# Another order for the first transfers on SyncE's queue in an attention and two-layer gated network kernel

## The chip, the cores and the metric

The kernel runs on one core of a Trainium2 chip. The time is the device time of one execution in microseconds (us); where several runs of a kernel are given, it is their median.

## What is computed

Attention over 4 batches of 8 heads (576 tokens, head size 64) with a block-causal mask, then a gated layer, then a mixture of four experts weighted by given probabilities. All inputs lie in the chip's memory; the three weights of the gated layer come as 64-bit floats and are turned into 32-bit ones on the chip.

```python
scores = scale * np.matmul(q, k.transpose(0, 1, 3, 2))
scores = np.where(mask, scores, -1000000000.0)         # blocks of 64, block_i >= block_j
scores = scores - np.max(scores, axis=-1, keepdims=True)
attn = np.exp(scores)
attn = attn / (np.sum(attn, axis=-1, keepdims=True) + 1e-09)
x = np.matmul(attn, v)                                 # (4, 8, 576, 64) -> (2304, 512)
gate = 1.0 / (1.0 + np.exp(-(x @ w_gate)))
x = gate * (x @ w_val) @ w_out
for e in range(4):
    out += p[:, e:e + 1] * (np.maximum(x @ w1[e], 0.0) @ w2[e])
```

## The kernel before, in words

TensorE does the products. Each 32-bit weight or activation is split into a high and a low part (`split_sb`, line 123), and three products of parts stand for one, so that a weight takes work on ScalarE, VectorE and GpSimd before TensorE can use it.

**Attention.** A batch has four pairs of heads. `attn_items` (line 151) writes the attention as one list of small steps, pair after pair. For a pair, `prep_tr` (line 220) transposes q and k on TensorE (lines 225, 233, 258), `s_begin` makes a score block (line 345), VectorE writes the mask and takes the row maximum (lines 375, 376; 406 and 408 for the last, short row block), ScalarE takes the exponentials (lines 378, 411), `p_tr` transposes them on TensorE (line 454) with ScalarE taking them out of PSUM (line 441), and `pv_both` multiplies with v into the tile `obank` (line 118, the helper that records these products) and stores the result (lines 532, 536).

**Weights of the gated layer.** They come in twelve groups of 128 columns. `conv_items` (line 628) gives twelve steps for a group: two loads of a raw block of 512 KB each (`raw`, line 634, one of `w_gate`, one of `w_val`), two conversions (`f64`, lines 601 on ScalarE, then 602 and 603 on VectorE), and then sums on GpSimd (line 649), splits (lines 128, 130, 132) and stores of the converted parts (line 657). The raw blocks have three buffers. Five groups (`NC0`, line 19) are converted while the attention of the first batch runs.

**Who loads what.** Nearly all transfers are issued by SyncE, one after the other, in the order in which the program writes them; an issue that has to wait for a buffer holds those behind it. ScalarE issues only the first pair's q. `load_first` (line 169) loads the first pair's q and k, with the last 64 tokens of both in two transfers of their own (line 176). `loads(g)` (line 203) loads the q and k of pair g in six transfers, and `load_v(g)` (line 207) its v in three (lines 195 and 199).

**What sets the order.** `attn_to(A00)` (lines 1283 and 1287) first writes the attention's list up to 12% of the first batch. `_merge` (line 43) then writes the rest of that batch and the weights' steps in alternation, so that both advance evenly. When the program has been written out, the compile step orders the instructions of each engine with a time model of its own (`TC_ARGS`, line 38): an instruction written later can go ahead of one whose inputs the model expects later. On the chip each engine runs its instructions in that fixed order. In the program of before, the first item of the list (line 552) issues `load_first`, `load_v(0)` and `loads(1)`; `load_v(1)` follows among the items up to 12%, and the raw blocks come only with `_merge`.

Of the kernel before, what the change touches and what calls it, by code (L numbers as in the profile page):

```python
# [18 lines left out]
NC0 = 5  # L19
# [9 lines left out]
PT2_BUFS = 1  # L29
LT, LP = 3, 4  # L30
PTB = 3
EARLY = True
HB = 19
W2B = 4
FIRSTP = 1
# [7 lines left out]
def _merge(a, b, pace=1.0):  # L43

    ta = sum(c for c, _ in a) or 1.0
    tb = sum(c for c, _ in b) or 1.0
    i = j = 0
    ca = cb = 0.0
    while i < len(a) or j < len(b):
        if j >= len(b) or (i < len(a) and pace * ca / ta <= cb / tb):  # L50
            c, fn = a[i]
            i += 1
            ca += c
        else:
            c, fn = b[j]
            j += 1
            cb += c
        fn()
# [3 lines left out]
def attention_moe_moe_kernel(  # L62
# [17 lines left out]
    E, _, F2 = w1.shape  # L80
# [3 lines left out]
    NF = DFF // P  # L84
# [66 lines left out]
    def attn_items(segs):  # L151
# [3 lines left out]
        items = []  # L155
# [4 lines left out]
        def nat_of(g):  # L160
            return pairs[g][3] != "F"

        def kts_of(g):
            return KTS[pairs[g][3]]
# [4 lines left out]
        def load_first():  # L169
            q0 = nat[0, "q"] = attn.tile([P, 5, 2, D], F32, tag="qn", name="qn")  # L170
            k0 = nat[0, "k"] = attn.tile([P, 5, 2, D], F32, tag="kn", name="kn")
            for c in range(4):
                for e, t, z in ((nc.scalar, q0, q), (nc.sync, k0, k)):
                    e.dma_start(out=t[:, c], in_=z[0, 0:2, c * P:(c + 1) * P, :].rearrange("h p d -> p h d"))
            for x, z in enumerate((k, q)):
                nc.sync.dma_start(
                    out=k0[64 * x:64 * x + 64, 4], in_=z[0, 0:2, 512:S, :].rearrange("h p d -> p h d"))

        def load(g, nm, src, c0, c1):
            _, b, pr, seg = pairs[g]  # L180
            if nm == "v":
                t = vts[g % 2]
            elif nat_of(g):
                if nm == "k" and pr % 2:
                    t = attn.tile([P, 5 * P], F32, tag="tk", name="kn", bufs=3)
                    t = t.rearrange("p (c h d) -> p c h d", c=5, h=2)
                else:
                    tag = "kn" if nm == "k" else ("qn", "vn")[pr % 2]
                    t = attn.tile([P, 5, 2, D], F32, tag=tag, name=f"{nm}n")
            else:  # L190
                t = attn.tile([P, 5, 2, D], F32, tag=f"{nm}n", name=f"{nm}n")
            nat[g, nm] = t

            for x, (y, z) in enumerate(((nm, src),) if nm == "v" else (("k", k), ("q", q)) if nm == "k" else ()):
                nc.sync.dma_start(
                    out=t[64 * x:64 * x + 64, 4], in_=z[b, 2 * pr:2 * pr + 2, 512:S, :].rearrange("h p d -> p h d"))
            cc = min(c1, 4)
            for h in range(2):
                nc.sync.dma_start(
                    out=t[:, c0:cc, h, :],  # L200
                    in_=src[b, 2 * pr + h, c0 * P:cc * P, :].rearrange("(c p) d -> p c d", p=P))

        def loads(g):
            load(g, "q", q, 0, 4)
            load(g, "k", k, 0, max(kts_of(g)) + 1)

        def load_v(g):
            load(g, "v", v, 0, max(kts_of(g)) + 1)
# [329 lines left out]
        def prep_list(g):  # L538
            seg = pairs[g][3]
            r = [(False, 0.0, lambda: prep_alloc(g))]  # L540
            for nm, cs in (("q", range(4)), ("k", KTS[seg])):
                for part in ([c for c in cs if c < 2], [c for c in cs if c >= 2]):
                    if part:
                        r.append((False, 110.0 * len(part), lambda nm=nm, part=part: prep_tr(g, nm, part)))
            return [(g, *x) for x in r]
# [3 lines left out]
        def later(s, *its):  # L549
            extra.setdefault(s, []).extend(its)  # L550

        items.append((0, False, 0.0, lambda: (load_first(), load_v(0), *((loads(1),) if EARLY and nat_of(1) else ()))))
        items += prep_list(0)
        for g in range(len(pairs)):
            if g == 0:
                continue
            base, per = start[g - 1], start[g] - start[g - 1]
            if g > 1 or not (EARLY and nat_of(1)):
                later(base, (g, False, 0.0, lambda g=g: loads(g)))
            later(base + per // 2, (g, False, 0.0, lambda g=g: load_v(g)))  # L560
            pl = prep_list(g)
            for m, it in enumerate(pl):
                later(min(base + per // 2 + (m * (per - 1 - per // 2)) // max(len(pl) - 1, 1), start[g] - 1), it)
# [31 lines left out]
    def from_f64(bits, out=None):  # L595

        lo, hi = bits[:, :, 0], bits[:, :, 1]
        f = lo if out is None else out.bitcast(I32)  # L600
        nc.scalar.activation(out=hi.bitcast(F32), in_=hi.bitcast(F32), func=AF.Prelu, scale=2.0 ** -112, alpha=2.0 ** 32)
        nc.vector.tensor_scalar(out=f, in0=lo, scalar1=29, scalar2=None, op0=ALU.logical_shift_right)  # L602
        nc.vector.scalar_tensor_tensor(  # L603
            out=f, in0=hi, scalar=3, in1=f, op0=ALU.logical_shift_left, op1=ALU.bitwise_or)
        return f.bitcast(F32)
# [19 lines left out]
    def w1_at(f, k):  # L625
        return wc_d[f][:, WAT[k][0] * QF:WAT[k][1] * QF].rearrange("p (h n f) -> p h n f", h=2, f=QF)

    def conv_items(f):

        d = {}  # L630

        def raw(gv):
            t = d["raw", gv] = conv.tile([P, NKT, P, 2], I32, tag="raw", name="raw", bufs=3)
            nc.sync.dma_start(
                out=t.rearrange("p c f t -> p c (f t)"),
                in_=(w_gate, w_val)[gv].bitcast(I32)[:, 2 * f * P:2 * (f + 1) * P].rearrange("(c p) f -> p c f", p=P))

        def f64(gv):
            d[gv] = from_f64(d["raw", gv].rearrange("p c f t -> p (c f) t"))

        def b(k, a):
            return d[a][:, k * QF:(k + 1) * QF]

        def sums(n):
            if n == 0:
                d["t"] = conv.tile([P, 4, QF], F32, tag="wt", name="wt")
            t = d["t"]
            x, y = [(b(0, 1), b(0, 0)), (b(1, 1), t[:, 0]), (b(1, 1), b(0, 1)), (b(1, 0), t[:, 1])][n]
            nc.gpsimd.tensor_tensor(out=t[:, n], in0=x, in1=y, op=ALU.subtract)

        def part(k):
            t = w1_tile(k)
            src = dict(a=lambda: d[0], b=lambda: d["t"][:, 0:2].rearrange("p n f -> p (n f)"),
                       c=lambda: d["t"][:, 2:4].rearrange("p n f -> p (n f)"), d=lambda: b(1, 1))[k]()
            split_sb(t[:, 0].rearrange("p n f -> p (n f)"), t[:, 1].rearrange("p n f -> p (n f)"), src,
                     "p" if k in "bc" else "a", "v" if k == "a" else "p")
            nc.sync.dma_start(out=w1_at(f, k), in_=t.bitcast(F32))
            if f >= NC0 - 1:
                wg[f, k] = t

        r = [lambda: raw(0), lambda: raw(1), lambda: f64(0), lambda: f64(1), lambda: sums(0), lambda: part("a"),
             lambda: sums(1), lambda: part("b"), lambda: sums(2), lambda: sums(3), lambda: part("c"), lambda: part("d")]
        return [(1.0, x) for x in r]
# [231 lines left out]
    if True:  # L895
# [380 lines left out]
        def attn_next():  # L1276
            queue[pos[0]][3]()
            pos[0] += 1
            if pos[0] == len(queue):
                pt2.release()  # L1280
                attn.release()

        def attn_to(target):
            while pos[0] < len(queue) and place[pos[0]] < target:
                attn_next()

        attn_to(A00)
        a0 = [(queue[i][2], attn_next) for i in range(pos[0], len(queue)) if place[i] < A1[0]]
        cs = [conv_items(f) for f in range(NF)]
        _merge(a0, sum(cs[:NC0], []), 1.0)  # L1290
        x_items = x1_prep(0)
        prev = []
        for p in range(NP1):
            at, total = 0.0, NF * 7 * 6 * C1 + NF * 2 * NKT * 3 * C1
            for f0 in range(0, NF, 2):
# [5 lines left out]
                items = []  # L1301
# [31 lines left out]
                if f0 == 0 and p < 2:  # L1333
                    items = x_items + items
# [22 lines left out]
        for p in range(NPASS):  # L1357
            for q0 in range(0, NQ, 2):
                last = p == NPASS - 1 and q0 == NQ - 2
                items = l1_items(p, q0) + l1_items(p, q0 + 1)  # L1360
                if (p, q0) == (0, 0):
                    m = len(items) // 2
                    items = [items[m * (c == "B") + "1526743".index(x)] for c, x in
                             ("A1", "A2", "A5", "B1", "A6", "B2", "A7", "B6", "B5", "A4", "B7", "A3", "B4", "B3")]
# [19 lines left out]
                if q0 == 0 and p:  # L1384
                    items = x_items[4:] + items
                if q0 == NQ - 2 and p + 1 < NPASS:
                    x_items = x_prep(p + 1)
                    items = x_items[:4] + items
# [41 lines left out]
```

## Time and profile before

| | us |
|---|---|
| median of 3 runs | 1418.28 |
| lowest and highest of them | 1415.96, 1418.3 |
| the profiled execution, its own time | 1414.19 |
| its span from first to last instruction | 1412.4 |
| TensorE busy in it | 1369.8 (97%) |
| VectorE busy | 981.4 (69%) |
| ScalarE busy | 780.9 (55%) |
| GpSimd busy | 505.2 (36%) |

In the rows PE is TensorE, PEld its weight loads, DVE VectorE, ACT ScalarE, POOL GpSimd and SP SyncE; a q behind the name (SPq) means the issuing of a transfer. L601 is line 601 of the kernel. "[3.28 <-DMA raw]" behind an instruction means that its engine had stood idle for 3.28 us until that transfer landed. Busy shares over the whole span say little about the opening, with which this change deals; it is read by stretches.

### The profile page before, as it was taken

How to read it: one execution, taken by the hardware profiler on the slowest of the kernel's cores; microseconds unless marked ns; L12 is line 12 of the kernel's file. 1: busy time of each engine (PE TensorE's matmuls, PEld its weight loads, DVE VectorE, ACT ScalarE, POOL GpSimd, SP SyncE). 2: the span in 40 equal slices, each digit the busy share in tenths (PEclk: the TensorE clock that was granted, in tenths of full speed). 3: DMA queues.
4: the chain of work that ended last, by engine and by line, in shares of the span. 5: the costliest groups of instructions: out<-in, count | busy, mean ns of one | idle time of the engine just before them, and what ended most of it. 6: DMA issues, size and time to landing. Idle time of an engine off the chain costs nothing.

```text
span 1412.4 us, 26270 instructions
## 1 busy us (share of the span) xinstructions
PE 1369.8 (97%) x9192; PEld 1264.0 (89%) x9192; DVE 981.4 (69%) x2111; ACT 780.9 (55%) x1926; POOL 505.2 (36%) x538
## 2 busy tenths in 40 slices
PE   5889998999999999999999999999999999999998
PEld 3447787888899999999999989999999999999998
DVE  6868689986666545567777666757766787766766
ACT  5878888888876433443445445444444454443442
POOL 4544357531112100022576556533322342322322
PEclk8999999999999999999999999999999999999999
DMA  8989787867656887898799888886666777776754
GB/s 230 314 239 297 224 262 253 261 197 211 214 183 227 305 298 264 291 368 306 270 333 359 295 304 298 293 297 237 232 245 247 254 263 282 245 270 229 277 203 157
DMA packets 213682, 371.91 MB, mean 263 GB/s; under 512 B 75568, under 2 KB 140080, under 8 KB 207408
## 3 DMA queue, kind: packets, MB, share of 16 engines
q1 hardware_dynamic: 212464, 369.99, 77.6%
q8 instruction: 73, 1.20, 0.3%
q14 instruction: 57, 0.47, 0.1%
q10 hardware_dynamic: 1088, 0.26, 0.1%
HBM read 269.00 MB, written 101.19 MB: 262 GB/s over the span
## 4 chain that ended last, share of the span: by engine, by line
PE 83%; DVE 6%; ACT 4%; DMA 3%; issue 1%; POOL 1%; SPq 1%; DVEq 0%; ACTq 0%; POOLq 0%
PE c L118 36%; PE o L118 26%; PE lo L118 6%; PE s L118 4%; PE obank L118 3%; PE t L118 3%; PE tbank L454 2%; PE s L345 1%; DMA raw<-in_moe_w_gate_dram 1%; DVE raw L602 1%; ACT pt L378 1%; DVE raw L603 1%; PE tbank L225 1%; DVE nm L376 1%; ACT pTb L441 1%
## 5 line engine op out<-in xcount | busy, mean ns | idle before, releaser
L118 PE MATMUL c<-xc,w1g 128*128 128x384 f32 x1920 | 384.8, 338 | 1.0 <-DMA w1g<-w1d 0.7
L118 PEld LDWEIGHTS c<-xc,w1g 128*128 128x128 f32 x1920 | 330.5, 188 | 7.5 <-issue 0.9
L118 PE MATMUL o<-w2s,hb 128*128 128x256 f32 x1728 | 243.5, 282 | 1.1 <-DVE acc L1207 1.1
L118 PEld LDWEIGHTS o<-w2s,hb 128*128 128x128 f32 x1728 | 231.8, 189 | 2.0 <-DVE acc L1207 1.7
L1067 POOL TENSOR_TENSOR hs<-hf 128x384 f32<-128x384 f32 x64 | 64.1, 1022 | 287.6 <-ACT hf L1075 256.5
L1207 DVE SCALAR_TENSOR_TENSOR acc<-o,pr_t,acc 128x256 f32<-128x256 f32 x264 | 123.5, 479 | 57.8 <-PE o L118 55.5
L118 PE MATMUL lo<-g,wo 128*128 128x288 f32 x888 | 147.2, 299 | 2.8 <-DVE x L880 2.8
L118 PE MATMUL o<-w,hb 128*128 128x512 f32 x576 | 142.9, 391 | 0.0
L118 PEld LDWEIGHTS lo<-g,wo 128*128 128x128 f32 x888 | 126.1, 188 | 6.6 <-DVE x L880 3.7
L1075 ACT ACTIVATE hf<-c 128x384 f32<-128x384 f32 x128 | 65.7, 514 | 114.3 <-DVE c L1112 57.6
L118 PEld LDWEIGHTS o<-w,hb 128*128 128x128 f32 x576 | 107.2, 188 | 18.5 <-DVE acc L1151 0.2
L1112 DVE TENSOR_TENSOR c<-c,snap 128x384 f32<-128x384 f32 x144 | 77.9, 553 | 55.7 <-PE c L118 36.5
L1105 ACT ACTIVATE snap<-c 128x384 f32<-128x384 f32 x144 | 65.8, 485 | 87.4 <-PE c L118 87.2
L1056 ACT ACTIVATE hb<-hs 128x384 fp32r<-128x384 f32 x128 | 63.3, 518 | 64.1 <-POOL hs L1067 64.0
L430 POOL TENSOR_SCALAR pt<-pt,nm 128x128 f32<-128x128 f32 (+4 forms) x72 | 47.3, 663 | 129.4 <-DVE nm L427 95.3
L1058 DVE TENSOR_TENSOR hb<-hs,hb 128x384 fp32r<-128x384 f32 x128 | 87.1, 695 | 5.5 <-ACT hb L1056 5.2
L880 DVE TENSOR_TENSOR x<-lo,x 128x288 f32<-128x288 f32 x124 | 55.6, 452 | 42.2 <-PE lo L118 41.7
L118 PE MATMUL c<-xc,wa 128*128 128x288 f32 x504 | 82.9, 299 | 2.1 <-ACT r L826 1.3
L378 ACT ACTIVATE pt<-s,nm 128x128 f32<-128x128 f32 (+3 forms) x128 | 67.6, 530 | 14.4 <-DVE nm L376 11.6
L118 PEld LDWEIGHTS c<-xc,wa 128*128 128x128 f32 x504 | 71.3, 188 | 4.2 <-ACT r L826 1.6
L118 PE MATMUL c<-xc,wc 128*128 128x288 f32 x432 | 71.1, 299 | 1.5 <-ACT snap L804 1.5
L454 PE MATMUL tbank<-ident,pt 128*128 128x128 f32 x320 | 55.1, 287 | 16.9 <-ACT pTa L441 9.6
(173 smaller groups left out, 2711.1 us busy)
## 6 DMA issues: line engine op xcount, KB each, us to landing
w1g<-w1d SPq DMA_DIRECT2D x96, 512.0 KB, 5.3
w2s<-w2d SPq DMA_DIRECT2D x48, 1024.0 KB, 6.3
w1d<-w1g SPq DMA_DIRECT2D x48, 512.0 KB, 5.3
wa<-w1d SPq DMA_DIRECT2D x40, 512.0 KB, 5.2
wb<-w1d SPq DMA_DIRECT2D x40, 512.0 KB, 5.4
wc<-w1d SPq DMA_DIRECT2D x40, 512.0 KB, 4.3
wo<-wod SPq DMA_DIRECT2D x36, 512.0 KB, 5.7
wr<-in_moe_w_dram SPq DMA_DIRECT2D x32, 512.0 KB, 5.5
```

What stands on the lines that cost most here:

```text
L118: ins = nc.tensor.matmul(out=out, lhsT=lhsT, rhs=rhs, start=start, stop=stop, skip_group_check=skip)
L378: ins = nc.scalar.activation(out=pt[:, x * nk:(x + 1) * nk], in_=sp[:, x - x0], func=AF.Exp, bias=nm[:, j0 + x:j0 + x + 1], scale=1.0, acc ...
L430: nc.gpsimd.tensor_scalar(out=p, in0=p, scalar1=nm[:, 2 + x:3 + x], scalar2=1.0, op0=ALU.mult, op1=ALU.mult)
L454: nc.tensor.transpose(out=tbank[:, x * P:(x + 1) * P], in_=pt[:, x * P:(x + 1) * P], identity=ident)
L880: nc.vector.tensor_tensor(out=x2[t, dm], in0=ps, in1=x2[t, dm], op=ALU.add)
L1056: nc.scalar.activation(out=t[:, 0], in_=src, func=AF.Copy if low is None else AF.Relu)
L1058: nc.vector.tensor_tensor(out=t[:, 1], in0=src, in1=t[:, 0].bitcast(F32), op=ALU.subtract)
L1067: nc.gpsimd.tensor_tensor(out=o, in0=x, in1=y, op=op)
L1075: nc.scalar.activation(out=hf[q, blk], in_=c, func=AF.Relu)
L1105: nc.scalar.activation(out=t, in_=d["c1"][:, :TH], func=AF.Copy)
L1112: nc.vector.tensor_tensor(out=c, in0=d[tag][:, :TH], in1=d[n], op=ALU.add)
L1207: nc.vector.scalar_tensor_tensor(out=o, in0=ps, scalar=pr, in1=o, op0=ALU.mult, op1=ALU.add)
```

## The change

Line 552 is split in two items: `load_first` alone, and then `loads(1)` with `load_v(0)` behind it instead of ahead. Between the two the two raw blocks of the first weight group are issued, and behind the second the first raw block of the second group. These three steps are then left out of the list that `_merge` distributes (57 steps instead of 60). The switch `EARLY` goes; it was on, so `loads(1)` stays where the first item was. SyncE's queue therefore begins with: the first pair's keys and last tokens, two raw blocks, the second pair's q and k, the first pair's v, a third raw block.

```diff
-        items.append((0, False, 0.0, lambda: (load_first(), load_v(0), *((loads(1),) if EARLY and nat_of(1) else ()))))
+        items.append((0, False, 0.0, load_first))
+        items.append((0, False, 0.0, lambda: (loads(1), load_v(0))))
...
-            if g > 1 or not (EARLY and nat_of(1)):
+            if g > 1:
                 later(base, (g, False, 0.0, lambda g=g: loads(g)))
...
+        cs = [conv_items(f) for f in range(NF)]
+        attn_next()
+        early = [cs[0][0], cs[0][1]]
+        for _, fn in early:
+            fn()
+        attn_next()
+        early.append(cs[1][0])
+        cs[1][0][1]()
         attn_to(A00)
         a0 = [(queue[i][2], attn_next) for i in range(pos[0], len(queue)) if place[i] < A1[0]]
-        cs = [conv_items(f) for f in range(NF)]
-        _merge(a0, sum(cs[:NC0], []), 1.0)
+        _merge(a0, [x for x in sum(cs[:NC0], []) if x not in early], 1.0)
```

## Rows read from the trace of the kernel before

**Rows 1.** Busy time by stretch: PE, PEld, DVE, ACT, POOL, then clock, DMA.
```profile
0.00:8.75 8.75, 3.92 (x15) 2.43 (x17) 2.12 (x8) 2.88 (x6) 1.78 (x10) 1.00 0.55 124
8.75:18.00 9.25, 6.23 (x30) 2.63 (x28) 5.09 (x19) 4.57 (x16) 0.00 (x0) 1.00 0.88 226
18.00:24.00 6.00, 0.42 (x2) 0.42 (x3) 5.43 (x13) 4.85 (x13) 4.48 (x6) 0.56 0.90 258
24.00:32.50 8.50, 7.40 (x34) 4.52 (x32) 7.68 (x14) 4.82 (x14) 7.20 (x8) 0.51 1.01 334
32.50:40.00 7.50, 7.17 (x43) 3.47 (x45) 7.22 (x21) 6.59 (x25) 5.89 (x6) 1.00 0.78 246
...
125.00:1413.00 1288.00, 1270.48 (x8597) 1205.00 (x8596) 891.22 (x1860) 687.45 (x1641) 442.24 (x462) 1.00 0.77 263
```

**Rows 2.** Chain of the latest releases in the first 24 us: start, length, what.
```profile
11.85 0.51 SPq L634
...
12.40 5.51 DMA raw<-in_moe_w_val_dram
...
17.93 0.70 ACT raw L601
```

**Rows 3.** SyncE's issues in order of time: start, length, line, tile.
```profile
3.96 0.60 SPq L176 DMA_DIRECT2D kn<-in_q_dram  x1
4.60 0.60 SPq L195 DMA_DIRECT2D vh<-in_v_dram  x1
5.25 1.15 SPq L199 DMA_DIRECT2D vh<-in_v_dram  x2
6.43 1.05 SPq L199 DMA_DIRECT2D qn<-in_q_dram  x2
...
8.83 1.14 SPq L199 DMA_DIRECT2D kn<-in_k_dram  x2
10.02 0.60 SPq L195 DMA_DIRECT2D vh<-in_v_dram  x1
...
12.40 0.51 SPq L634 DMA_DIRECT2D raw<-in_moe_w_val_dram  x1
...
17.69 0.51 SPq L634 DMA_DIRECT2D raw<-in_moe_w_gate_dram  x1
```

**Rows 4.** Instructions in order of time, the engines' first 30 us.
```profile
8.75 0.11 DVE L375 MEMSET s<- 64x64 f32 x1 [5.58 <-PE s L345]
...
11.65 0.51 PE L225 MATMUL tbank<-ident,qn 128*128 128x128 f32 x2
...
16.54 0.69 ACT L601 ACTIVATE raw<-raw 128x512 f32<-128x512 f32 x1 [2.31 <-DMA raw<-in_moe_w_gate_dram]
16.54 0.43 DVE L602 TENSOR_SCALAR raw<-raw 128x512 int32<-128x512 int32 x1 [3.28 <-DMA raw<-in_moe_w_gate_dram]
16.88 0.45 DVE L406 TENSOR_REDUCE nm<-s 128x1 f32<-128x288 f32 x1
...
19.43 2.00 POOL L649 TENSOR_TENSOR wt<-raw 128x256 f32<-128x256 f32 x2 [16.95 <-DVE raw L603]
...
22.38 0.66 ACT L601 ACTIVATE raw<-raw 128x512 f32<-128x512 f32 x1
...
23.58 0.90 PE L454 MATMUL tbank<-ident,pt 128*128 128x128 f32 x3 [8.33 <-ACT pTa L441]
...
24.42 1.55 PE L118 MATMUL obank<-pTa,vh 128*64 128x256 f32 x8
```

**Rows 5.** Time from issue to landing in the first 40 us: raw, then vh.
```profile
DMA to landing us min/median/max: 4.0/4.7/6.0
...
DMA to landing us min/median/max: 2.2/2.5/2.8
```

**Rows 6.** Busy time by stretches of 2.5 us, columns as in the first group.
```profile
5.00:7.50 2.50, 1.82 (x7) 1.01 (x6) 0.00 (x0) 0.56 (x3) 0.00 (x0) 1.00 0.46 104
7.50:10.00 2.50, 1.85 (x10) 1.13 (x12) 1.14 (x6) 1.37 (x7) 0.00 (x0) 1.00 0.71 159
10.00:12.50 2.50, 2.50 (x11) 1.15 (x13) 1.77 (x8) 1.37 (x7) 0.00 (x0) 1.00 0.70 160
12.50:15.00 2.50, 2.50 (x18) 1.20 (x14) 0.72 (x3) 1.73 (x6) 0.00 (x0) 1.00 0.92 219
15.00:17.50 2.50, 0.25 (x3) 0.01 (x1) 0.96 (x3) 0.69 (x1) 0.00 (x0) 1.00 1.13 348
```

**Rows 7.** Busy time where the last three batches' attention runs, columns as in the first group.
```profile
200.00:320.00 120.00, 110.88 (x804) 98.77 (x803) 107.00 (x276) 101.07 (x281) 65.76 (x75) 1.00 0.77 241
```

More of the change, by code (lines that the diff above doesn't have):

```diff
@@ L31 @@
 PTB = 3
-EARLY = True
 HB = 19
```

## The prediction, made blind

> **What bounds the kernel now.** I read the busy time by stretches first. Behind 125 us TensorE works 1270.48 of 1288 us [rows 1]: no earlier load gains there, but whoever arrives sooner ends sooner. The opening is another matter. From 18 to 24 us TensorE works 0.42 of 6 us, and from 24 to 32.5 us at a granted clock of 0.51, the lower of its two levels, 1.2 GHz [rows 1]. So I read the opening's instructions. The first softmax step begins at 8.75 us; TensorE's transposes at 23.58 us end 8.33 us of idle time [rows 4]. The reader is to see why: in that time VectorE and ScalarE stand before line 601/602, idle for 3.28 and 2.31 us until the first raw block lands at 16.54 us. The softmax step at 16.88 us (line 406) stands behind it in VectorE's fixed order and could not pass [rows 4]. The chain of the latest releases says the same: SyncE's issues in a row, then 5.51 us from the issue of the second raw block to its landing at 17.93 us, where its conversion begins [rows 2].
>
> From then on VectorE is the engine that has no room: 5.43 of 6, 7.68 of 8.5 and 7.22 of 7.5 us busy up to 40 us [rows 1], 20.33 of 22 us, 92%. TensorE waits there for what VectorE and ScalarE give it. A gain in the opening is therefore what VectorE wastes before 40 us and no longer wastes; TensorE's idle 8.33 us is not it, since the same VectorE work would still lie before TensorE.
>
> VectorE's waste from the first softmax on, 8.75 us: 9.25 - 5.09 = 4.16 us up to 18 us, and 22 - 20.33 = 1.67 us from there to 40 us [rows 1], in all 5.83 us. That is the **ceiling**.
>
> **The change part by part.** SyncE issues as much as before, in another order, so the sum of its issue times stays.
>
> *The two raw blocks.* They follow the last-token transfer that begins at 3.96 us [rows 3]. In their place stood v from 4.60 us on; so the first is issued at 4.60 instead of 11.85 us [rows 2, 3] and the second 0.55 us behind it, at 5.15 instead of 12.40 us [rows 3]: 7.25 us earlier each. The trace has no raw block among the first loads, so its landing is bounded by those that it shows: 4.0 to 6.0 us, median 4.7 [rows 5]. The first lands at 4.60 + 4.7 = 9.3 us (8.6 to 10.6), the second at 9.85 us (9.15 to 11.15). I take the median: the transfers' engines are 0.46 and 0.71 busy from 5 to 10 us, where the raw blocks now come, and were 0.92 and 1.13 busy where they were [rows 6]. Both land after the first softmax step can begin and well before the 13.26 us (16.54 - 3.28) at which VectorE today starts to wait for them [rows 4]. So the wait of 3.28 us goes. ScalarE's 2.31 us lies beside it and isn't counted again.
>
> What takes its place: the conversions can now stand ahead of the first softmax step, as they stand ahead of line 406 today [rows 4]. If so, VectorE waits from 8.75 to 9.3 us, 0.55 us (none if the order is kind; 1.85 us at the late bound of 10.6). Set against this are the small waits that move: of the 4.16 us, 0.88 us are not the wait for the block (4.16 - 3.28), and conversions in hand can fill them. I take them as filled in part, 0.55 us, which cancels. **Term: -3.3 us**; bounds -1.4 (3.28 - 1.85) and -5.8, the ceiling.
>
> *The second pair's q and k.* Six issues that took 6.43 to 9.97 us [rows 3] now begin behind the second raw block at 5.70 us: 0.73 us earlier. Their first reader is TensorE's transpose of q at 11.65 us [rows 4]. Cost nothing while they land by then. For the bound I give them the raw blocks' slowest landing instead of their own: 6.75 + 6.0 = 12.75 us (6.75 for the end of the two q issues, 5.70 + 1.05 [rows 3]), 1.1 us late. TensorE has idle time to give there, since VectorE comes last; taken as 0, up to +1.1.
>
> What the trace shows of sharing is that the second raw block's 5.51 us [rows 2] is above the median of 4.7 [rows 5], with the first block and a pair's loads around it. The Trainium skill (DMA: Bandwidth & Descriptors, "Two DMAs through the same engine are not ordered") has it that the pieces of transfers start in order within one queue of one transfer engine; that speaks against the change, as the small loads would stand behind 1 MB. By that rule the sum would be -3.3 + 1.1 = -2.2 us; no run here shows it yet. It is a rival below, at the price of the rows.
>
> *The first pair's v.* Three issues of 1.79 us together, from 4.60 [rows 3], now at 5.70 + 3.54 = 9.24 us behind the six of the second pair. Ended at 11.07 us, v lands by 13.9 us (2.8 [rows 5]), at a raw block's slowest by 17.1 us. Its reader is the product at 24.42 us [rows 4]; even 5.8 us earlier that is 18.6 us. Cost 0. The work that hides it is the whole first softmax; without that cover every us later would count.
>
> *The third raw block.* It goes out at about 11.1 instead of 17.69 us [rows 3] and lands by 17.1 us at 6.0. Today it lands at 22.4 us (17.69 + 4.7), just as ScalarE takes it at 22.38 us [rows 4]. Left where it was, it would cap the gain; with the change it doesn't up to 22.38 - 17.1 = 5.3 us. No term of its own, but the first term needs it.
>
> *What it is moved past.* The second pair's v goes out at 11.66 instead of 10.02 us [rows 3], with its reader far behind. GpSimd stands idle for 16.95 us until 19.43 us [rows 4] and can begin about 7 us sooner; its first groups then leave it waiting no longer than now.
>
> *The three steps fewer in the merged list.* Each conversion is written up to three steps earlier against the attention, fading to none at the end of the first batch. That reorders the opening and adds no work: 0, with the bounds in the first term and in the last rival.
>
> **Sum** -3.3 us. The profiled execution took 1414.19 us (span 1412.4 and 1.79 us around it); it would take 1410.9. The median of the runs is 4.09 us above it, and the change is counted in a stretch that all runs share: 1418.28 - 3.3 = **1415.0 us**. A measurement of this kernel can tell about 0.2%, 2.84 us, from no change; the sum lies just beyond.
>
> **The rivals.**
>
> *More comes back.* With the transposes no longer held, TensorE need not fall to 0.51 of its clock [rows 1], its products reach VectorE sooner and the 1.67 us of waste from 18 to 40 us go too. For it: the low clock follows right on the idle time. Against: VectorE is 92% busy there anyway. The ceiling, -5.8 us: 1412.5.
>
> *The block still comes late.* The conversions stand ahead of the first softmax and the block lands at the late bound: -1.4 us, 1416.9. For it: in the order of today VectorE waits 3.28 us for a block which that order expected sooner [rows 4]; a time model that errs so may err again. Against: the room on the transfers' engines [rows 6].
>
> *The second pair's loads stand behind the raw blocks*, and TensorE's transpose holds the scores behind it in its order: -2.2 us, 1416.1. For it: 1 MB is put ahead of them. Against: they are issued earlier than now and the engines have room.
>
> *It does not do what it says*: the order of SyncE's queue is left as it was by the compile step, 1418.3. Against: today's issues stand in the order in which they are written [rows 3].
>
> *Slower: the order drifts further down.* The compile step orders each engine by its own time model. From 200 to 320 us VectorE is 107.00 of 120 us busy and TensorE stands idle for 9.12 us [rows 7]. If the shifted opening changes the order there, so that the collisions double, 9.1 us come on top of the 3.3 saved: +5.8 us, 1424.1. It decides once such waits grow by over 3.3 us. For it: three steps fewer in a list that is spaced by shares. Against: the shift fades out before, and the work there is written by TensorE's progress.
>
> **How the numbers follow.** Chances: the forecast 0.47 (0.36 of it beyond 2.84 us), more comes back 0.16, the block late 0.14, the loads behind 0.09, not done 0.02, slower 0.12 (0.10 beyond 2.84 us; mild drift takes the rest). Faster by over 0.2%: 0.36 + 0.16 = 0.52. Slower: 0.10. Within: 0.38. The range runs from 1410.5 (the ceiling, and 2 us for the spread of 2.34 us between runs of before) to 1420.5 (no change, and the same 2 us).
>
> **What would show it.** Right: the first two raw blocks issued at 4.6 to 5.7 us and landed by 9 to 11 us; VectorE without a wait of over 1 us for a raw block; its busy share from 8.75 to 18 us up from 5.09 us [rows 1] to 8 us or more; GpSimd's first sum at 12 to 14 us; the first group of products (line 118 on v) some 3 us or more sooner than 24.42 us, and the same shift at 125 us. Wrong: a wait for q of the second pair at TensorE; a raw block that takes over 6 us; the shift there at 40 us and gone at 125 or 400 us, which would mean that something later had room for it.

## The result: slower, though the wait in the opening is gone

The changed kernel takes 1427.8 us (median of 6 runs) against 1418.25 us for the kernel before, run beside it: a ratio of 1.0072, 95% interval 1.0056 to 1.0089, or 9.5 us more. The profiled execution took 1431.84 us, the slowest of the six, with a span of 1429.9 us. In its lines the numbers below 552 are one lower than before's (line 344 is before's 345, 453 is 454, 117 is 118).

Busy time by stretch in the changed kernel, columns as in [rows 1]; the rows answer [rows 1] and [rows 7]:

```profile
8.75:18.00 9.25, 6.72 (x30) 2.80 (x28) 8.22 (x23) 6.49 (x19) 5.32 (x7) 1.00 1.15 276
18.00:24.00 6.00, 0.31 (x2) 0.32 (x3) 5.06 (x10) 3.32 (x9) 2.80 (x3) 0.82 0.83 213
24.00:32.50 8.50, 8.41 (x48) 4.99 (x47) 5.42 (x19) 6.61 (x23) 5.39 (x7) 0.73 1.00 345
...
200.00:320.00 120.00, 110.57 (x789) 97.34 (x788) 104.74 (x269) 100.00 (x275) 67.24 (x79) 0.99 0.74 234
125.00:1430.00 1305.00, 1278.63 (x8621) 1208.52 (x8620) 897.97 (x1869) 688.60 (x1655) 440.92 (x463) 1.00 0.76 260
```

SyncE's issues and the instructions of the opening in the changed kernel (start, length, engine and line), the answer to [rows 3] and [rows 4]:

```profile
4.74 0.59 SPq L634 DMA_DIRECT2D raw<-in_moe_w_gate_dram  x1
5.38 0.51 SPq L634 DMA_DIRECT2D raw<-in_moe_w_val_dram  x1
...
11.49 0.51 SPq L634 DMA_DIRECT2D raw<-in_moe_w_gate_dram  x1
```

```profile
8.62 0.43 DVE L602 TENSOR_SCALAR raw<-raw 128x512 int32<-128x512 int32 x1 [5.45 <-DMA raw<-in_moe_w_gate_dram]
9.06 0.11 DVE L374 MEMSET s<- 64x64 f32 x1
...
10.27 0.41 DVE L602 TENSOR_SCALAR raw<-raw 128x512 int32<-128x512 int32 x1
...
11.71 1.65 PE L344 MATMUL s<-tkn,tqn 64*128 64x384 f32 x4 [2.20 <-ACT pt L377]
...
12.59 1.64 POOL L649 TENSOR_TENSOR wt<-raw 128x256 f32<-128x256 f32 x2 [10.11 <-DMA vh<-in_v_dram]
...
23.69 0.90 PE L453 MATMUL tbank<-ident,pt 128*128 128x128 f32 x3 [6.02 <-ACT pTa L440]
...
24.52 1.12 PE L117 MATMUL obank<-pTa,vh 128*64 128x256 f32 x3
```

The first raw block lands at 8.62 us, 3.9 us after its issue (the other two that were moved take 4.7 and 4.8 us); VectorE's 3.28 us wait at 16.54 us [rows 4] is gone, and the 5.45 us in front of line 602 is idle time that stood before the first softmax step anyway (5.58 us, [rows 4]). GpSimd begins 6.8 us sooner. But the first product with v comes at 24.52 us, against 24.42 us before.

To see where time goes, I matched the products of TensorE in the two traces (the k-th of the same operation, tiles and shape) and took the difference of their starts, the median of each stretch of before's time. This **lag** is negative where the kernel leads. It is exact where the order is the same and blurred where it isn't; the changed kernel's last row equals the difference of the spans (1429.9 - 1412.4 = 17.5). Some 8 us of these 17.5 belong to the two executions that were traced, since the medians are only 9.5 us apart.

| before's time, us | changed | moved_old_order | new_order_to_72us | new_order_from_72us | new_order_to_100us | new_order_from_100us | new_order_to_400us | new_order_from_400us |
|---|---|---|---|---|---|---|---|---|
| 20-25 | 0.1 | -2.5 | -1.6 | -2.4 | -2.2 | -2.5 | -2.1 | -2.9 |
| 85-100 | -0.9 | -2.2 | -2.0 | -0.7 | -2.0 | -2.6 | -1.9 | -1.8 |
| 112-125 | 4.2 | -1.7 | 0.1 | 5.4 | 5.9 | 7.6 | 3.0 | -1.3 |
| 140-160 | 6.6 | -0.4 | 5.1 | 7.3 | 7.5 | 12.4 | 5.1 | -0.4 |
| 240-260 | 13.9 | -1.1 | 3.7 | 15.0 | 5.7 | 18.7 | 12.7 | -1.7 |
| 450-500 | 12.5 | -1.6 | 4.9 | 12.1 | 5.5 | 13.8 | 11.0 | 1.9 |
| 1000-1200 | 17.5 | -1.4 | 6.2 | 17.7 | 7.1 | 18.5 | 11.9 | 3.5 |

So the changed kernel leads by 1 to 2 us from 25 to 100 us, falls 7.5 us back between 100 and 160 us and some 6 more by 500 us. Each column is one execution and carries stalls of its own: the changed one's last 3 us come at 940 us and are absent in another kernel that has the same order there (one_exchange_back, 13.2 us at 800 and 13.3 us at 1000 us); that of new_order_to_72us loses 5 us at 140 us. What a change of order costs is therefore read from the timed runs.

One step is no accident of an execution. From 100-105 to 112-125 us the lag grows by 5.0 to 6.1 us in all six traces that have the changed kernel's orders on every engine there (changed, moved_sixty_steps, one_exchange_back, old_moves_new_order, new_order_from_72us, new_order_to_400us), and by 0.0 to 0.6 us in moved_old_order, one_exchange_forth, two_blocks_only and new_order_from_400us, which have before's (2.2 us in new_order_to_72us).

Compared with before, the compiled orders differ from VectorE's 9th instruction (8.8 us) on. On TensorE the last differing one is number 3345 of 8872; the longest stretch that can't be divided into equal sets runs from 611 to 2476. These are numbers of compiled instructions; the trace counts 9192 products, and in it the last differing one is number 3665, at 557 us of before's time, and the stretch runs from 151 to 439 us. The computation is the same.

### The profile page after: what moved, and what is told of

Its sections match the earlier page's. It is cut to its first block, busy times and chain, and to the rows that moved or that the text cites. A ratio compares the mean times of both kernels' runs of the same rounds, so it can differ in the third digit from the quotient of the medians.

```text
span 1429.9 us, 26265 instructions
## 1 busy us (share of the span) xinstructions
PE 1378.5 (96%) x9192; PEld 1267.1 (89%) x9192; DVE 982.5 (69%) x2111; ACT 779.1 (54%) x1926; POOL 501.7 (35%) x538
## 4 chain that ended last, share of the span: by engine, by line
PE 81%; DVE 6%; DMA 5%; ACT 3%; issue 2%; POOL 1%; SPq 1%; DVEq 0%; ACTq 0%; POOLq 0%
PE c L117 36%; PE o L117 24%; PE lo L117 7%; PE s L117 4%; PE obank L117 3%; PE t L117 3%; PE tbank L453 2%; PE s L344 1%; DMA raw<-in_moe_w_out_dram 1%; DMA w2d<-w2t 1%; DMA w1g<-w1d 1%; PE tbank L224 1%; DVE nm L375 1%; DMA raw<-in_moe_w_gate_dram 1%; ACT pt L377 1%
## 5 line engine op out<-in xcount | busy, mean ns | idle before, releaser
L117 PEld LDWEIGHTS o<-w,hb 128*128 128x128 f32 x576 | 107.2, 188 | 18.5 <-DVE acc L1151 0.3
L429 POOL TENSOR_SCALAR pt<-pt,nm 128x128 f32<-128x128 f32 (+4 forms) x72 | 44.4, 623 | 125.6 <-DVE nm L426 70.6
L804 ACT ACTIVATE snap<-c 128x288 f32<-128x288 f32 x108 | 44.1, 408 | 55.5 <-PE c L117 55.0
```

The lines of the kernel that those rows point to most:

```text
L117: ins = nc.tensor.matmul(out=out, lhsT=lhsT, rhs=rhs, start=start, stop=stop, skip_group_check=skip)
L429: nc.gpsimd.tensor_scalar(out=p, in0=p, scalar1=nm[:, 2 + x:3 + x], scalar2=1.0, op0=ALU.mult, op1=ALU.mult)
L804: nc.scalar.activation(out=t, in_=d["c1"][:, :TH1], func=AF.Copy)
```

## The experiments

Two theories stood against each other: **the transfers** lost (something lands late or collides), or **the orders** of the engines, which the compile step drew up anew, lost; within the second, the spacing of the list (57 instead of 60 steps) or the earlier loads as the time model sees them. To separate them I laid the orders down by hand: each instruction is tied, with no wait on the chip, to the one that is to stand ahead of it. `before[e]` and `after[e]` are the orders of engine e in the two kernels; `opening` is SyncE's order up to the third raw block.

### The transfers moved, every order as before; and the reverse

```diff
+out = dict(before)                       # moved_old_order
+first = opening(after["SP"])
+out["SP"] = first + [k for k in before["SP"] if k not in set(first)]
...
+out = dict(after)                        # old_moves_new_order
+first = opening(before["SP"])
+out["SP"] = first + [k for k in after["SP"] if k not in set(first)]
```

> SyncE's queue begins as in the changed kernel (keys, two raw blocks, second pair's q and k, first pair's v, third raw block); the order of the instructions on TensorE, VectorE, ScalarE and GpSimd, and of the rest of SyncE's queue, is laid down as in the kernel before. Theory 'order' (the loss comes from the new order that the compile step chose for the compute engines, far behind the opening; the transfers alone give part of the forecast): 1414 to 1418.5 us, ratio 0.997 to 1.000. Rival 'transfers' (the bulk put in front of the small loads, or the other timing of the transfers, costs the time): 1425 to 1429 us, ratio 1.005 to 1.0075. The blind forecast for this queue was 1415.0.

Measured: 1414.14 us, ratio 0.9976 (0.9954 to 0.9997), about -3.4 us.

> SyncE's queue begins as in the kernel before; the order of the instructions on the four compute engines, and of the rest of SyncE's queue, is laid down as in the changed kernel. Theory 'order': as slow as the changed kernel or slower, 1426 to 1436 us, since VectorE now also waits some 7 us for raw blocks that its order wants first. Rival 'transfers': 1417 to 1421 us.

Measured: 1432.4 us, ratio 1.0113 (1.0073 to 1.0153). So **the new orders lose** with either queue: 1.0072 / 0.9976 = 1.0096, some 13.6 us with the moved transfers (by the two intervals, 10 to 17 us). In the new orders the moved transfers make no difference that is clear of the noise: the intervals of 1.0113 and 1.0072 overlap. In the traces the four compute engines run moved_old_order in before's order throughout and old_moves_new_order in the changed kernel's. moved_old_order is faster than both kernels. Its opening (lines 609 and 610 are before's 601 and 602, 458 is 454):

```profile
11.71 0.63 PE L229 MATMUL tbank<-ident,qn 128*128 128x128 f32 x2
...
13.24 0.42 DVE L610 TENSOR_SCALAR raw<-raw 128x512 int32<-128x512 int32 x1
...
16.95 2.01 POOL L657 TENSOR_TENSOR wt<-raw 128x256 f32<-128x256 f32 x2 [14.45 <-DVE raw L611]
...
21.10 0.88 PE L458 MATMUL tbank<-ident,pt 128*128 128x128 f32 x3 [4.67 <-ACT pTa L445]
...
21.91 1.55 PE L122 MATMUL obank<-pTa,vh 128*64 128x256 f32 x8
```

Line 610 no longer waits and runs 3.30 us sooner than before's 16.54 us; the products with v come 2.51 us sooner, and the lead is 2.2 us before 100 us and 1.4 us at the end of this execution.

### Two blocks without the third

```diff
+two = [sp[i] for i in raws(sp)[:2]]
+first = sp[:6] + two                     # before's orders otherwise
+out["SP"] = first + [k for k in sp if k not in set(first)]
```

> All compute orders as in the kernel before; only the first group's two raw blocks go out ahead of the first pair's v, and the third block stays at its old place behind the third pair's loads. By the blind working the third block then lands at about 22 us and caps the gain: ScalarE waits for it at line 601 for some 1 to 2 us and the lead at 60 us shrinks from 2.2 us to 0.5 to 1.5 us, 1415 to 1418 us. If the third block is hidden anyway the lead at 60 us stays 2.2 us.

Measured: 1417.11 us, ratio 0.999 (0.9977 to 1.0003). The wait has only moved to the third block, and the product with v is back at its old place (24.60 us):

```profile
22.57 0.90 DVE L610 TENSOR_SCALAR raw<-raw 128x512 int32<-128x512 int32 x1 [1.65 <-DMA raw<-in_moe_w_gate_dram]
```

### The spacing of the list

```diff
-        _merge(a0, [x for x in sum(cs[:NC0], []) if x not in early], 1.0)
+        _merge(a0, [(1.0, lambda: None) if x in early else x for x in sum(cs[:NC0], [])], 1.0)   # moved_sixty_steps
...
+        for _, fn in early: fn()         # spacing_alone: line 552 as before, the three loads at the list's head
```

> The transfers are moved as in the changed kernel, but the three steps leave empty places in the list that is spread over the attention (60 steps, not 57), so that the conversions are written where they were before; the compile step orders the engines itself. Theory 'order by the time model': the model sees the blocks land earlier and moves conversions ahead all the same, 1424 to 1430 us. Rival 'spacing' (the three steps fewer shift the list and cause the loss): 1414 to 1418.5 us.

Measured: 1428.49 us, ratio 1.0074 (1.0043 to 1.0105), as the change itself. In its trace the four compute engines and SyncE's issues stand in the order of the changed kernel from the first to the last instruction: 57 or 60 steps make no difference here, and the moved loads alone bring the new orders.

> The other half: SyncE's queue begins nearly as in the kernel before (v and the second pair's loads first, then the three raw blocks together at the head of the spread list), and the list has 57 steps. Rival 'spacing': 1425 to 1429 us. Theory 'order by the time model': the order changes only up to about the 526th product on TensorE (some 110 us), so 1416 to 1421 us.

Measured: 1423.76 us, ratio 1.0029 (1.0012 to 1.0047), outside both ranges. The run isn't the spacing alone, since its third raw block goes out at 12.96 us instead of 17.69 us. It costs some 4 us with orders that differ only up to about 146 us. So another draw of the orders can cost here too; the change's loss does not hang on the spacing.

### The new orders cut in two

With the moved transfers throughout, one kernel's orders up to a cut and the other's behind it. The first three labels hold for VectorE. On TensorE each cut falls later, because its numbers count compiled instructions and not the trace's products. By the traces, in us of before's time:

| label | TensorE | VectorE | ScalarE |
|---|---|---|---|
| 72us | 94 to 107 | 72 | 69 to 70 |
| 100us | 125 | 98 | 94 |
| 127us | 151 | 127 | 118 to 119 |
| 400us | 440 to 441 | 428 | 441 to 494 |

Where a range is given, the two orders agree within it.

```diff
+a, b = (after, old) if NEW_FIRST else (old, after)
+out[e] = a[e][:CUT[e]] + b[e][CUT[e]:]   # for every engine e; old = moved_old_order's
```

> Transfers moved. The changed kernel's orders up to some 72 us (conversions ahead of the first softmax), the orders of the kernel before behind that. Theory 'late' (the loss is made by the new orders behind 72 us): the opening's order costs about the 1.3 us by which the two traces differ at 60 us, so 1414.5 to 1417.5 us, ratio 0.997 to 1.000. Rival 'opening' (putting the conversions ahead of the first softmax sets all that follows back): 1424 to 1429 us.

Measured: 1414.39 us, ratio 0.9973 (0.9961 to 0.9986).

> Transfers moved. The orders of the kernel before up to some 72 us, the changed kernel's behind that. Theory 'late': nearly as slow as the changed kernel, 1424 to 1428 us, ratio 1.004 to 1.007. Rival 'opening': 1413 to 1417 us.

Measured: 1426.35 us, ratio 1.0058 (1.0039 to 1.0078). The opening's new order costs nothing that can be measured; **the loss lies behind this cut**, at 69 us or later, and so far behind the opening, whose transfers the change moves.

> Transfers moved. The orders of the kernel before up to some 127 us, the changed kernel's behind that. By the lag of the changed kernel's products behind those of the kernel before (some 5 us at 125 us, 12 at 300 us): theory 'spread' (the new orders cost in several places) gives 1417 to 1422 us, ratio 0.999 to 1.003. Rival 'one place' (all is lost between 72 and 127 us, and later lag is its echo): 1413 to 1416 us. Rival 'VectorE's full stretch' (all is lost from 127 to 320 us): 1424 to 1428 us.

Measured: 1444.31 us, ratio 1.0197 (1.017 to 1.0224), slower than either parent and outside what every theory gave. Between 118 and 151 us it has ScalarE, then VectorE, in the new order while TensorE still follows the old one, a mixture that neither kernel has. It has waits of its own (from 70 to 330 us TensorE stood 9.6 us for transposed exponentials that ScalarE takes out of PSUM at line 445, one of these waits 7.2 us long), so this cut says nothing about the place.

> The changed transfers; every engine's order is that of the changed kernel up to about 100 us (449 of TensorE's instructions, 194 of VectorE's, 164 of ScalarE's) and that of the kernel before behind it. The theory that the loss begins in the stretch from 100 to 125 us, where the new order puts ScalarE's split of a GpSimd sum ahead of a softmax exponential, expects 1414 to 1416 us, as with the cut at 72 us. The rival that the new orders already spoil something between 72 and 100 us which shows only later expects 1420 to 1428 us.

Measured: 1423.9 us, ratio 1.0042 (1.0028 to 1.0056): neither theory's number for the first, and above the 1414.39 of the cut at 72 us.

> The reverse cut: orders of the kernel before up to about 100 us, those of the changed kernel behind it. If the loss begins behind 100 us: 1425 to 1429 us, as with the cut at 72 us. If it hangs on the orders from 72 to 100 us: 1414 to 1418 us. A cut that breaks a pairing, as the one at 127 us did, would give over 1435 us.

Measured: 1435.39 us, ratio 1.0119 (1.009 to 1.0147), again slower than both parents. Both kernels lose in the first 40 us behind the cut, by 9.5 and 15 us in the table of lags. This pair of runs, too, has TensorE in one order from 98 to 125 us and VectorE and ScalarE in the other, so they don't tell how the loss divides between the cuts.

> The changed transfers; the orders of the changed kernel up to about 400 us (2476 of TensorE's instructions, 892 of VectorE's, 839 of ScalarE's, 177 of GpSimd's), those of the kernel before behind it. If the loss is all made by 260 us, as the lag against the kernel before suggests (13.9 us at 240 to 260 us, 12.5 at 450 to 500 us): 1426 to 1430 us. If the orders behind 400 us make it: 1414 to 1417 us. If it is shared: 1420 to 1424 us.

Measured: 1426.41 us, ratio 1.0058 (1.0038 to 1.0079).

> The reverse cut: orders of the kernel before up to about 400 us, those of the changed kernel behind it. If the loss is all made by 260 us: 1413 to 1416 us, as with the old orders throughout. If the orders behind 400 us make it: 1425 to 1430 us. If it is shared: 1418 to 1423 us.

Measured: 1418.87 us, ratio 1.0002 (0.9985 to 1.002). The larger part is made before this cut: 1.0058 / 0.9976 = 1.0082, some 12 us (8 to 16). The orders behind it (or the cut itself) come to 1.0002 / 0.9976 = 1.0026, 3.7 us, which the intervals don't tell from nothing (-0.2 to 7.6); that kernel's lag shows a step from -1.7 to 1.9 us by 450 us.

### One exchange at 110 us

In the changed kernel ScalarE has the split of a GpSimd sum ahead of a softmax exponential at 110.78 us, and TensorE's scores wait behind both; in before the exponential stands first. Changed kernel:

```profile
110.78 0.44 ACT L129 ACTIVATE xc<-xs 128x288 fp32r<-128x288 f32 x1 [2.30 <-POOL xs L714]
...
111.83 0.70 PE L344 MATMUL s<-tkn,tqn 64*64 64x288 f32 x4 [1.49 <-ACT pt L377]
```

```diff
+l[i], l[i + 1] = l[i + 1], l[i]          # ScalarE: split and exponential change places
```

> The changed kernel with one exchange on ScalarE at about 111 us: the softmax exponential goes ahead of the split of GpSimd's sum, as in the kernel before. If this exchange carries the step from 108 to 114 us (about 4 us of lag), the time is 1422 to 1425 us and the wait of 2.30 us there no longer holds TensorE's scores. If it is one of many exchanges that each cost little: 1426 to 1429 us, as the changed kernel.

Measured: 1426.78 us, ratio 1.0059 (1.0042 to 1.0075). The exponential goes first, and waits as long, now for VectorE's row maximum:

```profile
109.69 0.58 ACT L382 ACTIVATE pt<-s,nm 128x384 f32<-128x384 f32 x1 [2.20 <-DVE nm L380]
...
110.41 0.70 PE L349 MATMUL s<-tkn,tqn 64*64 64x288 f32 x4 [1.82 <-ACT pt L382]
```

> The changed transfers with the orders of the kernel before, and the same exchange made the other way: the split of GpSimd's sum goes ahead of the softmax exponential at about 108 us. If the exchange by itself costs: 1416 to 1420 us, 2 to 5 us above the same kernel without it (1414 us). If it costs only with what surrounds it in the changed orders: 1413 to 1415 us.

Measured: 1417.06 us, ratio 0.9983 (0.9971 to 0.9995). The time lies in the first range, but the ratio lies within moved_old_order's interval, 1.0 us above it, so a cost of the exchange by itself isn't shown. In either direction it carries at most a small part of the loss. one_exchange_back also shows that laying the orders down by hand costs nothing that can be measured: it has the changed kernel's orders in all but this place, and its time.

What the trace does show is what happens on TensorE from 100 to 130 us. Busy time by stretch, columns as in [rows 1]; first the changed kernel, then moved_old_order:

```profile
100.00:130.00 30.00, 27.17 (x149) 18.33 (x148) 21.66 (x57) 22.82 (x65) 16.12 (x17) 0.82 0.70 213
...
110.00:115.00 5.00, 3.16 (x21) 1.78 (x20) 4.09 (x10) 4.22 (x12) 1.66 (x2) 0.89 0.80 198
115.00:120.00 5.00, 5.00 (x31) 4.36 (x30) 1.56 (x4) 3.02 (x8) 3.96 (x4) 0.76 0.92 308
```

```profile
100.00:130.00 30.00, 28.81 (x193) 20.69 (x194) 24.52 (x65) 25.23 (x75) 15.05 (x16) 0.95 0.85 262
...
110.00:115.00 5.00, 4.00 (x29) 3.05 (x27) 4.20 (x7) 4.20 (x13) 3.66 (x5) 1.00 0.90 254
115.00:120.00 5.00, 4.81 (x31) 3.68 (x32) 3.64 (x11) 4.75 (x19) 2.61 (x3) 1.00 1.09 324
```

In the same 30 us TensorE does 149 products instead of 193, VectorE works 21.66 instead of 24.52 us, and the granted clock is 0.82 instead of 0.95. From 110 to 120 us of each kernel's own time the clock is below full speed in all six traces that have the step of 5 to 6 us (0.83 in the changed kernel, 0.66 to 0.83 in four others, 0.92 in old_moves_new_order), and 1.00 in before, moved_old_order, one_exchange_forth, two_blocks_only, new_order_to_72us and new_order_from_400us. Which exchanges of order bring it about isn't shown.

TensorE's busy time can hide such a loss, since a product at the lower clock counts as longer busy (the changed kernel's products with v of 128x320 take 0.76 us each from 100 to 104.9 us and 0.45 us from 130 to 160 us, at 0.50 and 1.00 of the clock): from 100 to 107.5 us it is busy all the time in both kernels, with 35 and 50 products.

```profile
100.00:102.50 2.50, 2.50 (x8) 0.75 (x6) 0.89 (x4) 1.94 (x6) 1.44 (x2) 0.50 0.05 11
102.50:105.00 2.50, 2.50 (x12) 1.42 (x12) 1.74 (x6) 1.75 (x6) 0.29 (x1) 0.50 0.00 0
105.00:107.50 2.50, 2.50 (x15) 1.60 (x11) 2.42 (x6) 1.80 (x6) 2.50 (x3) 0.58 0.27 111
```

```profile
100.00:102.50 2.50, 2.50 (x11) 1.46 (x12) 1.85 (x6) 1.74 (x5) 0.74 (x1) 0.50 0.02 4
102.50:105.00 2.50, 2.50 (x21) 1.59 (x17) 1.80 (x6) 2.07 (x8) 2.29 (x3) 0.88 0.48 184
105.00:107.50 2.50, 2.50 (x18) 1.79 (x17) 2.48 (x9) 1.53 (x4) 0.27 (x1) 1.00 0.90 315
```

The first fence is the changed kernel, the second moved_old_order. Both fall to 0.50 (1.2 GHz) behind a stretch in which TensorE worked little (0.72 of 2.5 us from 95 us, 0.71 of 2.5 us from 92.5 us); the changed one stays there longer. This difference is one of executions and does not carry the loss: moved_sixty_steps, with the changed kernel's orders, runs at 1.00 here, and new_order_to_72us stays low (0.57 from 100 to 107.5 us) and is as fast as moved_old_order in the timed runs.

## Why the prediction was wrong, point by point

**The two blocks: right.** Issued at 4.74 and 5.38 us (4.60 and 5.15 foreseen), the first landed at 8.62 us, the early bound of the range given. The term of -3.3 us stands measured at -3.4 us (-6.5 to -0.4) with the orders of before, and at -3.8 us (-5.5 to -2.0) with the new opening. The wait is gone as foreseen and the size fits, but so closely by luck: the intervals are wide, and in its trace moved_old_order leads by only 2.2 us before 100 us.

**The second pair's q and k: right, 0.** With the orders of before (moved_old_order) their first transpose runs at 11.71 us and waits for nothing, against 11.65 us [rows 4]. The order of pieces that the Trainium skill states (DMA: Bandwidth & Descriptors, "Two DMAs through the same engine are not ordered") costs nothing here: the loads are there in time, whether or not they stood behind the blocks.

**v and the third block: right.** No product waits for v; without the third block the gain is gone (ratio 0.999), as the working said.

**The three steps fewer ("That reorders the opening and adds no work: 0"): the step that failed.** It took the list's spacing for what re-orders the engines, let that end with the opening and put it at nothing. With sixty places kept the orders are the changed kernel's all the same, and so is the loss (1.0074): the moved loads are enough. How the compile step comes from them to its orders isn't shown. The orders differ up to 557 us, not within the opening, and cost some 13.6 us.

**The rival "the order drifts further down"** was the case that came, with too small a chance (0.12), too small a price (9.1 us against 13.6), and another place. Its mark, TensorE's idle time from 200 to 320 us, grew from 9.12 us [rows 7] to only 9.43 us. The argument against it, that the shift fades out before, speaks of the list, which changed no order here; the orders that the compile step drew up go on differing.

**The marks** of a right prediction: four of five held in a kernel that is slower, VectorE's missing wait with the remark made on line 602 above. VectorE's 8.22 us from 8.75 to 18 us passes the 8 us asked for, and misleads: some 0.6 us of it is an instruction that took over twice its time (below). Only the fifth mark, the products with v 3 us sooner and the same at 125 us, answers the question; they were 0.10 us later, and at 112 to 125 us 4.2 us behind. In moved_old_order they came 2.51 us sooner, and still 1.7 us at 125 us. Of the signs of being wrong, two showed: a shift of 1.4 us at 40 to 60 us that is gone at 125 us, and a later raw block, issued at 20.54 us, that took 7.4 us to land.

**A slip in the range**: by its own words the upper end is 1418.28 + 2 = 1420.28, not 1420.5. 1427.8 lies above either.

**What stays open**: which exchanges of order between the first cut and the last (from some 70 to 440 us) make the loss. Of its 13.6 us, 5 to 6 are made between 100 and 112 us of before's time, in every trace with the new orders there; where the rest is made isn't shown. The cuts at 100 and 127 us mix the two orders across engines, and the one exchange that was tried is not it.

## What to carry to other kernels

Where a compile step orders the engines by a model, moving a load changes two things: when data lands, and every order that follows from it; price them apart. Here the second was the larger, 13.6 us against 3.4. Test them apart by holding the orders: here that turned 9.5 us lost into about 3.4 us gained. Before you read a cut of one order into another, look up in the trace where it falls on each engine. Judge a gain in the opening by its lead at a later point, not by a wait that is gone.

## What the runs showed of the hardware

I had not expected VectorE's instructions to take up to 1.63 us where the same ones take 0.43, 0.69 and 0.67 us earlier in the same trace (at 8.62, 9.35 and 10.91 us, while GpSimd stands idle). In the changed kernel, VectorE first, then GpSimd beside it:

```profile
16.36 1.03 DVE L602 TENSOR_SCALAR raw<-raw 128x512 int32<-128x512 int32 x1 [0.19 <-DMA raw<-in_moe_w_gate_dram]
17.49 1.57 DVE L603 SCALAR_TENSOR_TENSOR raw<-raw 128x512 int32<-128x512 int32 x1
...
19.80 1.63 DVE L131 TENSOR_TENSOR wa<-raw,wa 128x512 fp32r<-128x512 f32 x1 [0.18 <-ACT wa L129]
```

```profile
16.36 0.75 POOL L649 TENSOR_TENSOR wt<-raw,wt 128x256 f32<-128x256 f32 x1
17.06 1.45 POOL L131 TENSOR_TENSOR wb<-wt,wb 128x512 fp32r<-128x512 f32 x1
...
19.62 1.26 POOL L131 TENSOR_TENSOR wc<-wt,wc 128x512 fp32r<-128x512 f32 x1
```

Each ends a little after a GpSimd instruction that was running: 17.39 after 17.11 us, 19.06 after 18.51, 21.43 after 20.88, so 0.28, 0.55 and 0.55 us later, each time 0.12 to 0.15 us less than its usual length, as if nearly all of it had run only then. Against 0.43, 0.69 and 0.67 us the three cost 2.4 us in all. The Trainium skill (SBUF — State Buffer, "Who interferes with whom") says that VectorE and GpSimd share a pair of ports which one holds for a whole instruction; these ends agree with it. In the run of new_order_to_72us, which has the same orders here, VectorE's three begin 0.16, 0.13 and 0.03 us ahead of GpSimd's and take 0.48, 0.72 and 0.68 us; there two of GpSimd's are the longer, 0.91 and 1.73 us against 0.75 and 1.45 us. The product with v came at 22.82 us, 1.7 us sooner than in the changed kernel. Of the six traced kernels with the moved transfers and the new opening order, three have the first product with v at 24.5 to 24.8 us (changed, moved_sixty_steps, one_exchange_back) and three at 22.2 to 22.8 us (new_order_to_72us, new_order_to_100us, new_order_to_400us). So GpSimd's earlier start, counted at nothing in the prediction, can take VectorE's time in the stretch where VectorE has no room; no run changed it alone. It is not the change's loss: new_order_from_72us has before's opening order and loses as much.
